# One written order for five engine queues over the first seven attention cycles of a fused attention, layer-norm, MLP and token-mixing kernel

## The chip, the core and the metric

The kernel runs on one core of a Trainium2 chip. The core has a matrix engine (PE, with its weight loads PEld), a vector engine (DVE), an activation engine (ACT), a slower general engine (POOL) and a queue engine (SP) that issues loads and stores. Each engine takes its instructions in the order of its own queue; an instruction that needs the result of another engine waits on a semaphore. The metric is device time in microseconds (us); the median of several runs of the changed kernel is set against 537.79 us.

## What is computed

```python
# attention, 2 batches x 8 heads x 768 positions x 64, fp32
scores = q @ k.T / 8 + bias            # keep: first n_global=8 keys, or the last n_local=96
a = exp(scores - max) / (sum + 1e-9)
x = (a @ v), heads side by side        # 2 x 768 x 512
# layer norm and MLP
x = x + relu(layernorm(x) * g @ w_ch1) @ w_ch2          # 512 -> 2048 -> 512
# mixing
theta = x @ w_theta;  z = x*cos(theta), x*sin(theta)
u = x + w_tok_r @ z_r + w_tok_i @ z_i
out = u + relu(u @ w_ch)
```

All inputs are 32-bit floats, but the weights reach the kernel as 64-bit words in an array `wall`, 58 pieces of 128x512; each piece has to be decoded into a 32-bit tile and then split into a high and a low part for the matrix products of the MLP.

## The kernel before

The 1536 positions are 12 blocks of 128 (`SEQ`, in the order 1, 2, 3, 4, 5, 7, 8, 0, ...). A loop over cycles `t` works on several blocks at once: cycle `t` makes the scores of block `t`, the value product of block `t-1` and its layer norm, and, from cycle 3 on, two hidden tiles of the MLP. So each cycle puts on PE two halves of the scores (`s<-k,q`), four transposes of the probabilities (`pt<-ident,e`), one value product (`xa<-pts,v`), a transpose back (`xp`), one of the normalized block (`xnp`), two hidden products (`hp`) and two output products (`op`). On DVE stand the row maxima (line 229, which adds the bias and keeps the maximum), half of the copies of `pt` to `pts` (line 275), the softmax scale (L311), the layer norm (L323 to L331), the low parts (L341, L438) and two steps of decoding (L374, L375). On ACT stand the exponentials (L236), the other half of the copies (L273), the lift of `xa` (L298), the high parts (L340, L396, L438) and the two other steps of decoding (L369, L373). POOL makes the low parts of the first eight split weight pieces (L397). All heads of a block have to be through maximum, exponential, transpose and copy before its value product can begin.

Eight weight pieces, those of the first four hidden tiles, are decoded and split within the first six cycles (`NPIECES`). From cycle 7 on the loop is the same in both kernels.

What sets the order: in `tc.manual_schedule(engines={...})` the named engines take their instructions as the program is written. In this loop that is PE alone; for DVE, ACT, POOL and SP a scheduler picks at build time, by its own estimates, among what is ready, held by a few hints such as

```python
with tc.issue_after(lifted) if t else ExitStack():
    soften_(t, HI)                       # maxima and exponentials of heads 4 to 7
pieces(want[0])                          # behind_exp: decode behind the last exponential
```

PE starts with 11 products on zeros (`spin`, line 87), and eight more stand in cycle 0 (`idle`, `idle0b`, `idle0c`, from `SPINS`). The bias tiles are made in `make_bias`: a chain of eight DVE steps (L170 to L178), then one scaled copy for each head, two on DVE (`DVE_BIAS`, L183) and six on ACT (L185).

Of the kernel before, what the change touches and what calls it, by code (L numbers as in the profile page):

```python
# [12 lines left out]
U32 = mybir.dt.uint32  # L13
AF = mybir.ActivationFunctionType
# [3 lines left out]
P = 128  # L18
# [25 lines left out]
def kernel(ctx, tc, q, kwin, v, n_pair, g_ln, wall, out):  # L44
# [45 lines left out]
    make_identity(nc, ident)  # L90
# [62 lines left out]
    def make_bias(old):  # L153
# [24 lines left out]
        v_.scalar_tensor_tensor(rel, key, nl, rel, ALU.subtract, ALU.max)  # L178
        for h in range(H):
# [6 lines left out]
        yield  # L186
# [35 lines left out]
    def soften(b, i, p, e, s):  # L222

        nk = e.shape[-1]
        b0 = 0 if i else WIN
        nm, sm = stat[b, i]
        for j in range(2):
# [5 lines left out]
            maxima.append(r.ins)  # L233
        for j in range(2):
# [3 lines left out]
        e_t[b, i, p] = e  # L238

    def scores(b, i, ps_):  # L240

        nk = WIN if i else P
        if ps_[0] == 0:
# [14 lines left out]
    def soften_all(b, i, ps_, s):  # L258
        for a, p in enumerate(ps_):
            e = at.tile([P, 2, s[0].shape[-1]], F32, tag="p", name=f"e{b}_{i}_{p}", bufs=NE)  # L260
            soften(b, i, p, e, [s[j][:, a, :] for j in range(2)])

    def flip_probs(b, i, p):
        nb = 2 if i else 1
        e = e_t.pop((b, i, p))
        pt_tag = "m" if p % 2 else "pt"
        pt = ps(pt_tag, [P, 2, nb, P], f"pt{b}_{i}_{p}")
# [3 lines left out]
        pts = at.tile([P, 2, nb, P], F32, tag="pt", name=f"pts{b}_{i}_{p}", bufs=NPT)  # L271
        if p % 2 == 0:
# [3 lines left out]
        pts_t[b, i, p] = pts  # L276

# [71 lines left out]
    n_staged, n_decoded = [0], [0]  # L349
# [10 lines left out]

    def decode(i, out):

        n = n_decoded[0]
        n_decoded[0] += 1
        load_to(n)
        assert order[n] == i
        r = stage.pop(i)
        load_to(n + NRAW)
        nc.scalar.activation(out, r.bitcast(F32)[:, :, 1], AF.Copy, scale=2.0**-112)  # L369
        t = rawp.tile([P, DM], I32, tag="dec", name=f"dec{i}", bufs=1)  # L370
        o = out.bitcast(I32)
        if i >= 0:
            nc.scalar.activation(t, r.bitcast(U32)[:, :, 0], AF.Copy, scale=2.0**-29 * (1 - 2.0**-15), bias=-0.4999)  # L373
            nc.vector.scalar_tensor_tensor(t, o, 3, t, ALU.logical_shift_left, ALU.bitwise_or)  # L374
            nc.vector.scalar_tensor_tensor(o, r[:, :, 1], -2**31, t, ALU.bitwise_and, ALU.bitwise_or)  # L375
            return
        nc.vector.tensor_scalar(t, o, 3, None, ALU.logical_shift_left)
        nc.vector.scalar_tensor_tensor(t, o, -2**31, t, ALU.bitwise_and, ALU.bitwise_or)
        nc.vector.scalar_tensor_tensor(o, r[:, :, 0], 29, t, ALU.logical_shift_right, ALU.bitwise_or)
# [8 lines left out]
    def split_w(f, ds=(0, 1)):  # L388
        decode_to(2 * f + ds[-1] + 1)
        r = split_t.setdefault(f, [])  # L390
        for d in ds:
            nm = ("w1", "w2")[d]
            s = piece[2 * f + d]
            hi = ws.tile([P, DM], F32R, tag=f"{nm}h", name=f"{nm}h{f}", bufs=GROUP)
            lo = ws.tile([P, DM], F32R, tag=f"{nm}l", name=f"{nm}l{f}", bufs=GROUP)
            nc.scalar.activation(hi, s, AF.Copy)  # L396
            (nc.vector if f >= GROUP else nc.gpsimd).tensor_tensor(lo, s, hi.bitcast(F32), ALU.subtract)  # L397
            r += [hi, lo]
# [5 lines left out]
    def make_xt(t):  # L404
        c, ts = chunk_of[t]
        if c % 2 == 0 and t == ts[0]:
            xt_t[c // 2] = [slot(f"xt{x}{c}") for x in "hl"]
        at_ = c % 2 * CW + ts.index(t) * P
        sl = slice(at_, at_ + P)
        hi, lo = xt_t[c // 2]  # L410
        transposed(xn_t.pop(t), hi[:, :, sl], lo[:, :, sl], "h", f"xnp{t}")
# [5 lines left out]
    def mlp_h(c, f, tag, part=None):  # L417
# [6 lines left out]
        wh, wl = split_t[f][0:2]  # L424
        if part != 1:
            hp_t[c, f] = ps(tag, [P, cn], f"hp{c}_{f}")
        hp = hp_t[c, f]
        kks = range(KD) if part is None else range(part * KD // 2, (part + 1) * KD // 2)
        n = 3 * kks[0]
        for kk in kks:  # L430
# [4 lines left out]
        if part == 0:  # L435
            return
        hh, hl = (act.tile([P, 2 * CW], F32R, tag=f"h{x}", name=f"h{x}{c}_{f}", bufs=2)[:, 0:cn] for x in "hl")
        r = nc.scalar.activation(hh, hp, AF.Relu), nc.vector.scalar_tensor_tensor(hl, hp, 0.0, hh.bitcast(F32), ALU.max, ALU.subtract)  # L438
        relus.append([x.ins for x in r])
        ht_t[c, f] = (hh, hl)  # L440

# [6 lines left out]
    def mlp_o(c, f, fs, js=range(4)):  # L448
# [4 lines left out]
        wh, wl = split_t[f][2:4]  # L453
        for j in js:
# [4 lines left out]
            if f == fs[-1]:  # L459
# [228 lines left out]
    def general():  # L688
# [61 lines left out]
        n_staged[0] = n_decoded[0] = 0  # L750
# [66 lines left out]
    nloaded = [0]  # L817

    def loads_to(n):
        while nloaded[0] <= min(n, len(blocks) - 1):  # L820
            b, i = blocks[nloaded[0]]
            load_qk(b, i)
            load_v(b, i)
            nloaded[0] += 1

    loads_to(0)
    warm = keep.tile([P, 1], F32, name="warm")
    nc.scalar.activation(warm, nhalf, AF.Exp)
    bias_steps = make_bias(True)
    next(bias_steps)  # L830
    next(bias_steps)
    loads_to(1)
    load_to(0)
# [17 lines left out]
    def flips(t, ps_):  # L851
        if 0 <= t < NB:
# [3 lines left out]
    made = []  # L856

    def pieces(n):
        if len(made) < n:
            with behind_exp(len(maxima) - 1):  # L860
                while len(made) < n:
                    m = len(made)
                    split_w(m // 2, (m % 2,))
                    made.append(m)

    sc = {}

    def score(t, ps_):
        if t < NB and (t, ps_) not in sc:
            sc[t, ps_] = scores(*blocks[t], ps_)  # L870

    def soften_(t, ps_):
        if (t, ps_) in sc and sc[t, ps_]:
            soften_all(*blocks[t], ps_, sc[t, ps_])
            sc[t, ps_] = None

    LO, HI = (0, 1), (2, 3)
    with tc.manual_schedule(engines={mybir.EngineType.PE}):
        spin("m", "spin", SPIN0)
        for t in range((LEAD + len(items)) // 2 + 1):  # L880
            j = 2 * t - LEAD
            sp = SPINS[t] if t < len(SPINS) else (0, 0, 0)
            want = NPIECES[min(t, len(NPIECES) - 1)]
            loads_to(t + 2)
            score(t, LO)
            score(t, HI)
            soften_(t, LO)
            if 0 <= t - 1 < NB:
# [3 lines left out]
            with tc.issue_after(lifted) if t else ExitStack():  # L892
# [161 lines left out]
```

## Time and profile before

| | |
|---|---|
| median of three runs | 537.79 us (537.69 to 537.82) |
| profiled execution: its own time | 537.6 us |
| profiled execution: span of the trace | 535.8 us |
| PE busy | 522.2 us, 97% of the span |
| DVE, ACT, POOL busy | 361.0, 284.3, 19.6 us |
| granted clock of PE, mean | 0.999 |

The span runs from the first to the last instruction in the trace; the 1.8 us between it and the time of that execution lie around it. The three runs lie within 0.13 us. A trace time counts from the start of the span.

### The profile page before, as it was taken

The page shows a single profiled execution, that of the slowest core. Times are in us where ns is not written, and L with a number is a line of the kernel's source. Part 1 is how long each engine was busy: PE and PEld are TensorE (multiplying, and loading weights), DVE is VectorE, ACT ScalarE, POOL GpSimd, SP SyncE. Part 2 cuts the span into 40 slices and gives each one's busy share as a digit, 9 for nine tenths or more (in the row PEclk, how much of TensorE's full clock was granted, in tenths as well). Part 3 has the DMA queues.
Part 4 walks back from the last instruction along what each step waited for, and adds up shares of the span by engine and source line. Part 5 has one row for each costly group of instructions (what it writes and reads, how often), then busy time and mean ns, then how long its engine had stood idle before and what let it go on. Part 6 is the DMA issues. An engine that isn't in the chain of part 4 may idle for free.

```text
span 535.8 us, 8220 instructions
## 1 busy us (share of the span) xinstructions
PE 522.2 (97%) x3091; PEld 439.7 (82%) x3091; DVE 361.0 (67%) x789; ACT 284.3 (53%) x631; POOL 19.6 (4%) x32
## 2 busy tenths in 40 slices
PE   8779999999999999999999999999999999999996
PEld 3567889888888888888888887788888888888886
DVE  5898786977774445355468776995996689821532
ACT  6888665667652323332346557972885666620200
POOL 0223100000000000000000000000000000000000
PEclk9999999999999999999999999999999999999999
DMA  8975632312131232012324343221400000000122
GB/s 276 372 236 178 207 110 98 108 53 80 40 120 38 82 105 89 3 40 78 119 78 157 117 159 119 86 72 39 157 2 1 1 0 1 1 1 20 59 81 83
DMA packets 18831, 49.11 MB, mean 92 GB/s; under 512 B 2272, under 2 KB 4576, under 8 KB 18784
## 3 DMA queue, kind: packets, MB, share of 16 engines
q1 hardware_dynamic: 18496, 47.98, 26.4%
q8 instruction: 26, 0.43, 0.3%
q10 hardware_dynamic: 288, 0.52, 0.3%
q14 instruction: 21, 0.17, 0.1%
HBM read 45.35 MB, written 3.15 MB: 91 GB/s over the span
## 4 chain that ended last, share of the span: by engine, by line
PE 90%; ACT 5%; DVE 3%; issue 1%; DMA 1%; ACTq 0%; DVEq 0%
PE op L458 24%; PE hp L433 24%; PE acc L633 19%; PE thm L556 6%; PE ch L679 6%; PE pt L270 3%; PE xa L289 3%; PE s L255 2%; ACT e L236 2%; PE xp L339 1%; PE xp L310 1%; PE xnp L339 1%; DVE w L375 1%; DMA words<-in_n 1%; DVE e L229 1%
## 5 line engine op out<-in xcount | busy, mean ns | idle before, releaser
L633 PE MATMUL acc<-tokh,z 128*128 128x256 f32 (+1 forms) x384 | 95.5, 336 | 0.0
L438 ACT ACTIVATE hh<-hp 128x512 fp32r<-128x512 f32 (+1 forms) x60 | 30.5, 508 | 101.7 <-PE hp L433 101.5
L433 PE MATMUL hp<-xth,w1h 128*128 128x512 f32 (+1 forms) x240 | 84.2, 351 | 0.0
L433 PE MATMUL hp<-xtl,w1h 128*128 128x512 f32 (+1 forms) x240 | 83.2, 347 | 0.0
L433 PE MATMUL hp<-xth,w1l 128*128 128x512 f32 (+1 forms) x240 | 83.1, 346 | 0.0
L458 PE MATMUL op<-w2h,hh 128*128 128x512 f32 x192 | 76.9, 400 | 0.0
L458 PE MATMUL op<-w2l,hh 128*128 128x512 f32 x192 | 75.0, 390 | 0.0
L458 PE MATMUL op<-w2h,hl 128*128 128x512 f32 x192 | 74.8, 392 | 0.0
L633 PEld LDWEIGHTS acc<-tokh,z 128*128 128x128 f32 x384 | 66.6, 190 | 7.9
L438 DVE SCALAR_TENSOR_TENSOR hl<-hp,hh 128x512 fp32r<-128x512 f32 (+1 forms) x60 | 34.7, 579 | 56.3 <-ACT hh L438 56.2
L633 PE MATMUL acc<-tokl,z 128*128 128x512 f32 (+1 forms) x192 | 64.6, 336 | 0.0
L236 ACT ACTIVATE e<-e,nm 128x256 f32<-128x256 f32 (+1 forms) x96 | 45.8, 479 | 15.1 <-DVE nm L229 15.1
L433 PEld LDWEIGHTS hp<-xth,w1h 128*128 128x128 f32 x240 | 45.2, 188 | 7.9 <-ACT e L236 0.9
L433 PEld LDWEIGHTS hp<-xtl,w1h 128*128 128x128 f32 x240 | 45.3, 189 | 6.2 <-DVE xtl L341 0.2
L433 PEld LDWEIGHTS hp<-xth,w1l 128*128 128x128 f32 x240 | 45.3, 189 | 5.6
L458 PEld LDWEIGHTS op<-w2h,hl 128*128 128x128 f32 x192 | 36.0, 188 | 8.5 <-DVE hl L438 0.9
L458 PEld LDWEIGHTS op<-w2l,hh 128*128 128x128 f32 x192 | 36.1, 188 | 6.6
L458 PEld LDWEIGHTS op<-w2h,hh 128*128 128x128 f32 x192 | 36.1, 188 | 6.5
L373 ACT ACTIVATE dec<-raw 128x512 int32<-128x512 uint32 x58 | 38.3, 661 | 4.5 <-DVE chr L375 1.7
L633 PEld LDWEIGHTS acc<-tokl,z 128*128 128x128 f32 x192 | 36.4, 190 | 4.1
L229 DVE CUSTOM_DVE_ANT_0 e<-s,bias 128x256 f32<-128x256 f32 (+1 forms) x96 | 32.4, 395 | 6.0 <-PE s L255 6.0
L446 DVE SCALAR_TENSOR_TENSOR x2all<-op,rsall,x2all 128x512 f32<-128x512 f32 x48 | 33.3, 741 | 2.1 <-PE op L458 2.1
(142 smaller groups left out, 889.4 us busy)
## 6 DMA issues: line engine op xcount, KB each, us to landing
raw<-in_wall SPq DMA_DIRECT2D x58, 512.0 KB, 3.5
k<-in_kwin SPq DMA_DIRECT2D x9, 512.0 KB, 5.2
vc<-in_v SPq DMA_DIRECT2D x12, 256.0 KB, 4.2
q<-in_q SPq DMA_DIRECT2D x11, 256.0 KB, 4.1
out<-o SPq DMA_DIRECT2D x8, 256.0 KB, 2.0
vw<-in_v SPq DMA_DIRECT2D x10, 192.0 KB, 5.2
out<-o SPq DMA_DIRECT2D x8, 128.0 KB, 1.8
vw<-in_v SPq DMA_DIRECT2D x10, 64.0 KB, 4.9
```

The source lines that it names most:

```text
L229: r = nc.vector.tensor_tensor_reduce(out=e[:, j, :], in0=s[j], in1=bias[h][:, b0:b0 + nk], scale=-SCALE, scalar=3.0e38, op0=ALU.add, op1=A ...
L236: r = nc.scalar.activation(e[:, j, :], e[:, j, :], AF.Exp, bias=nm[:, h:h + 1], scale=-1.0, accum_out=sm[:, h:h + 1])
L270: nc.tensor.transpose(pt[:, j, c, :], e[:, j, c * P:(c + 1) * P], ident)
L289: nc.tensor.matmul(xa[j * D:(j + 1) * D, p, :], vv[:, h * D:(h + 1) * D], pts[:, j, c, :], start=(c == 0), stop=(c == nb - 1),)
L373: nc.scalar.activation(t, r.bitcast(U32)[:, :, 0], AF.Copy, scale=2.0**-29 * (1 - 2.0**-15), bias=-0.4999)
L433: nc.tensor.matmul(hp, l, r[:, kk, :], start=(n == 0), stop=(n == 3 * KD - 1))
L438: r = nc.scalar.activation(hh, hp, AF.Relu), nc.vector.scalar_tensor_tensor(hl, hp, 0.0, hh.bitcast(F32), ALU.max, ALU.subtract)
L446: nc.vector.scalar_tensor_tensor(x2[t], o, rsall[:, t:t + 1], x2[t], ALU.mult, ALU.add)
L458: nc.tensor.matmul(op_t[c][j], l, r, start=(f == fs[0] and n == 0), stop=(f == fs[-1] and n == 2))
L556: nc.tensor.matmul(mp, l[:, kk, :], r[:, kk, :], start=(n == 0), stop=(n == 3 * KD - 1))
L633: mm = nc.tensor.matmul(o, l[:, dsl], r[:, sl], start=first and not (paired and d % 2), stop=end and not (paired and d % 2 == 0))
L679: nc.tensor.matmul(mp, l[:, kk, es], r, start=(kk == 0 and m == 0), stop=(kk == KD - 1 and m == 2))
```

## The change

The loop over the first seven cycles is replaced by a list of 283 units, `ORDER`, and all five queues take their instructions in the order of this list. The code of these cycles is cut into the functions that the units name. The letters that the text below uses: S half of a block's scores, M and E maxima and exponentials of two heads, F transpose and C copy of two heads (the last letter of a C says whether ACT, `s`, or DVE, `v`, copies), V value product, L lift, K inverse sum, X transpose back, Y scale, N and J layer norm, T, H and W transpose and high and low part of the normalized block, A, B, D and G the four decoding steps (ACT, ACT, DVE, DVE), I and P high part (ACT) and low part (POOL) of a weight piece, U hidden product, h and l its high and low part, O output product, g its addition to the block, q and v loads, b and f bias steps. The digit behind a letter is the cycle, block, piece or hidden tile; `V3` is the value product of the fourth block in `SEQ`.

```diff
-    make_identity(nc, ident)
...
-DVE_BIAS = 2
-FIRST = 5
-EARLY = 1
-NPIECES = [(0, 1), (1, 3), (3, 5), (5, 8), (8, 8)]
+DVE_BIAS = 4
-SPINS = [(4, 2, 2)]
+ORDER = """
+S00 b0 b3 b1 b2 S01 Z4 M00 E00 M03 M02 E03 F00p M01 S11 E02 C00v E01 F03o M12 F02m C03v F01p C02s K0 E12 S10 C01v
...
@@ make_bias @@
+        nc.gpsimd.iota(rel[:, own], [[-1, P]], base=0, channel_multiplier=1, **io)
         if old:
...
-        nc.gpsimd.iota(rel[:, own], [[-1, P]], base=0, channel_multiplier=1, **io)
...
+    def decode_high(i, out):
+        decode_part(i)["out"] = out
+        nc.scalar.activation(out, stage[i].bitcast(F32)[:, :, 1], AF.Copy, scale=2.0**-112)
+
+    def decode_low(i):
+        t = decode_part(i)["low"] = rawp.tile([P, DM], I32, tag="dec", name=f"dec{i}", bufs=1)
+        nc.scalar.activation(t, stage[i].bitcast(U32)[:, :, 0], AF.Copy, scale=2.0**-29 * (1 - 2.0**-15), bias=-0.4999)
+
+    def decode_merge(i):
+        out, t = (dec_t[i][x] for x in ("out", "low"))
+        nc.vector.scalar_tensor_tensor(t, out.bitcast(I32), 3, t, ALU.logical_shift_left, ALU.bitwise_or)
+
+    def decode_sign(i):
...
+        load_to(order.index(i) + NRAW)
+        nc.vector.scalar_tensor_tensor(out.bitcast(I32), r[:, :, 1], -2**31, t, ALU.bitwise_and, ALU.bitwise_or)
...
-    loads_to(0)
+    qk_to(1)
+    v_to(0)
...
+    with tc.manual_schedule(engines={ET.DVE, ET.Pool}):
+        next(bias_steps[True])
+        make_identity(nc, ident)
+        next(bias_steps[True])
+    with tc.manual_schedule(engines={ET.SP}):
+        load_to(0)
+        qk_to(2)
+        v_to(1)
+        load_to(1)
+        nc.sync.dma_start(gbc, g_ln.partition_broadcast(P))
+        v_to(2)
+        load_to(2)
...
+    with tc.manual_schedule(engines={ET.PE, ET.Activation, ET.DVE, ET.Pool, ET.SP}):
+        spin("m", "spin", SPIN0)
+        for token in ORDER.split():
+            UNITS[token[0]](*[int(x) if x.isdigit() else x for x in token[1:]])
...
     with tc.manual_schedule(engines={ET.PE}):
-        spin("m", "spin", SPIN0)
-        for t in range((LEAD + len(items)) // 2 + 1):
+        for t in range(FIRST, (LEAD + len(items)) // 2 + 1):
```

`FIRST` is 7 in the last line. Three places show what moved. The first is ACT at the start. `bias` tiles are scaled copies, `e` the probabilities of a block and a pair of heads, `warm` a first exponential on one column. Before:

```order
L828 ACTIVATE warm<-nhalf 128x1
L185 ACTIVATE bias_102<-biasTrue_121 128x256
L185 ACTIVATE bias_103<-biasTrue_121 128x256
L185 ACTIVATE bias_104<-biasTrue_121 128x256
L185 ACTIVATE bias_105<-biasTrue_121 128x256
L185 ACTIVATE bias_106<-biasTrue_121 128x256
L185 ACTIVATE bias_107<-biasTrue_121 128x256
L236 ACTIVATE e_1_0_195,sm_1_182<-e_1_0_195,nm_1_181 128x256 x2
```

and now:

```order
L911 ACTIVATE warm<-nhalf 128x1
L193 ACTIVATE bias_100<-biasTrue_123 128x256
L193 ACTIVATE bias_101<-biasTrue_123 128x256
L193 ACTIVATE bias_102<-biasTrue_123 128x256
L193 ACTIVATE bias_103<-biasTrue_123 128x256
L251 ACTIVATE e_1_0_211,sm_1_185<-e_1_0_211,nm_1_184 128x256 x2
L251 ACTIVATE e_1_3_216,sm_1_185<-e_1_3_216,nm_1_184 128x256 x2
```

Two copies of the bias have left ACT for DVE, and the second pair of heads that goes through is pair 3. The second place is ACT around the lift of the first block (`xs_1`), with the second block's probabilities (`e_2`) and the first two weight pieces (`w`, `dec`, `w1h`). Before:

```order
L298 ACTIVATE xs_1_321<-xa_1_304 128x512
L396 ACTIVATE w1h_291<-w_279 128x512
L236 ACTIVATE e_2_2_323,sm_2_236<-e_2_2_323,nm_2_235 128x256 x2
L236 ACTIVATE e_2_3_328,sm_2_236<-e_2_3_328,nm_2_235 128x256 x2
L273 ACTIVATE pts_2_0_354<-pt_2_0_349 128x512
L369 ACTIVATE w_386<-raw_280 128x512
L373 ACTIVATE dec_390<-raw_280 128x512
L273 ACTIVATE pts_2_2_368<-pt_2_2_363 128x512
```

and now:

```order
L251 ACTIVATE e_2_0_302,sm_2_233<-e_2_0_302,nm_2_232 128x256 x2
L321 ACTIVATE xs_1_318<-xa_1_285 128x512
L251 ACTIVATE e_2_3_280,sm_2_233<-e_2_3_280,nm_2_232 128x256 x2
L251 ACTIVATE e_2_1_310,sm_2_233<-e_2_1_310,nm_2_232 128x256 x2
L292 ACTIVATE pts_2_3_354<-pt_2_3_337 128x512
L292 ACTIVATE pts_2_0_360<-pt_2_0_329 128x512
L411 ACTIVATE w_367<-raw_159 128x512
L292 ACTIVATE pts_2_1_377<-pt_2_1_362 128x512
```

The split of the first weight piece (`w1h`) no longer stands between the lift and the exponentials; it comes more than twenty rows later, and ACT copies three pairs of this block. The third place is PE between the first and the second value product (`xa_1`, `xa_2`). Before:

```order
L289 MATMUL xa_1_304<-pts_1_3_268,vc_1_114 64x128 x2
L310 MATMUL xp_335<-ident,xs_1_321 128x128 x4
L270 MATMUL pt_2_0_349<-ident,e_2_0_243 128x128 x4
L270 MATMUL pt_2_1_356<-ident,e_2_1_248 128x128 x4
L270 MATMUL pt_2_2_363<-ident,e_2_2_323 128x128 x4
L270 MATMUL pt_2_3_370<-ident,e_2_3_328 128x128 x4
L339 MATMUL xnp_379<-ident,xn_345 128x128 x4
L255 MATMUL s_3_0_0_421<-k_3_173,q_3_172 128x256
```

and now:

```order
L312 MATMUL xa_1_285<-pts_1_3_259,vc_1_114 64x128 x2
L285 MATMUL pt_2_2_313<-ident,e_2_2_251 128x128 x4
L337 MATMUL xp_322<-ident,xs_1_318 128x128 x4
L285 MATMUL pt_2_0_329<-ident,e_2_0_302 128x128 x4
L285 MATMUL pt_2_3_337<-ident,e_2_3_280 128x128 x4
L269 MATMUL s_3_0_0_348<-k_3_151,q_3_150 128x256
L269 MATMUL s_3_0_1_349<-k_3_151,q_3_150 128x256
L269 MATMUL s_3_0_0_348<-k_3_151,q_3_150 128x256
L269 MATMUL s_3_0_1_349<-k_3_151,q_3_150 128x256
L285 MATMUL pt_2_1_362<-ident,e_2_1_310 128x128 x4
L376 MATMUL xnp_372<-ident,xn_356 128x128 x4
```

A transpose of probabilities stands ahead of the transpose back (`xp`), and half of the third block's scores ahead of the last transpose and of `xnp`.

## Rows read from the trace of the kernel before

**Rows 1.** The page: busy time, share of the span and instructions of PE.

```profile
PE 522.2 (97%) x3091; PEld 439.7 (82%) x3091; DVE 361.0 (67%) x789; ACT 284.3 (53%) x631; POOL 19.6 (4%) x32
```

**Rows 2.** Stretches between value products: start:end, length, busy by engine, clock, DMA, GB/s.

```profile
15.55:26.17 10.62, 7.73 (x74) 6.03 (x73) 9.28 (x25) 9.30 (x25) 2.81 (x3) 1.00 1.04 374
26.17:37.00 10.83, 7.79 (x74) 6.03 (x73) 10.10 (x31) 9.44 (x28) 3.11 (x4) 1.00 0.67 226
37.00:48.81 11.81, 11.45 (x104) 9.70 (x103) 10.34 (x33) 9.67 (x28) 2.62 (x4) 1.00 0.56 190
48.81:62.15 13.34, 12.50 (x110) 10.87 (x108) 11.65 (x35) 9.29 (x27) 4.68 (x6) 1.00 0.63 198
62.15:74.44 12.29, 12.29 (x110) 10.85 (x109) 10.11 (x37) 7.29 (x25) 0.55 (x1) 1.00 0.31 109
...
84.80:535.80 451.00, 446.37 (x2471) 380.30 (x2470) 292.28 (x566) 221.57 (x447) 4.04 (x6) 1.00 0.20 68
```

**Rows 3.** Waits of PE from 5.98 to 84.80: us, times, longest.

```profile
PE xp L310 <- ACT xs L298: 3.1, 3, 1.5
PE pt L270 <- ACT pts L273: 3.0, 3, 1.7
```

**Rows 4.** Two stretches that begin with the first maximum and first exponential.

```profile
7.14:48.81 41.67, 34.72 (x295) 25.72 (x291) 35.95 (x117) 36.57 (x106) 8.54 (x9) 1.00 0.81 282
8.36:48.81 40.45, 33.50 (x286) 25.11 (x284) 34.73 (x111) 35.35 (x102) 8.54 (x9) 1.00 0.80 280
```

**Rows 5.** Waits of ACT from 8.36 to 48.81.

```profile
ACT w2h L396 <- DVE w L375: 2.4, 3, 1.4
ACT e L236 <- DVE nm L229: 1.6, 2, 0.8
```

**Rows 6.** Timeline of DVE and ACT at the start: begin, us, operation.

```profile
4.50 0.22 DVE L170 TENSOR_SCALAR biasTrue<-biasTrue 128x128 f32<-128x128 f32 x1
...
5.08 0.35 DVE L175 TENSOR_SCALAR biasTrue<-biasTrue,nval 128x256 f32<-128x256 f32 x1
...
6.45 0.50 DVE L183 TENSOR_SCALAR bias<-biasTrue 128x256 bf16<-128x256 f32 x2
7.14 0.42 DVE L229 CUSTOM_DVE_ANT_0 e<-s,bias 128x256 f32<-128x256 f32 x1 [0.20 <-PE s L255]
...
6.51 1.95 ACT L185 ACTIVATE bias<-biasTrue 128x256 bf16<-128x256 f32 x6 [3.35 <-DVE biasTrue L178]
8.36 0.49 ACT L236 ACTIVATE e<-e,nm 128x256 f32<-128x256 f32 x1
```

**Rows 7.** Timeline of POOL and DVE where a split meets a decoding step.

```profile
25.20 1.28 POOL L397 TENSOR_TENSOR w2l<-w,w2h 128x512 fp32r<-128x512 f32 x1 [3.09 <-ACT w2h L396]
...
25.72 1.30 DVE L374 SCALAR_TENSOR_TENSOR dec<-w,dec 128x512 int32<-128x512 int32 x1
...
27.29 0.68 DVE L375 SCALAR_TENSOR_TENSOR w<-raw,dec 128x512 int32<-128x512 int32 x1
```

**Rows 8.** Timeline of PE: units of a cycle, and the start of cycle 7.

```profile
64.05 0.39 PE L433 MATMUL hp<-xth,w1h 128*128 128x256 f32 x1
...
65.58 0.60 PE L310 MATMUL xp<-ident,xs 128*128 128x128 f32 x4
...
72.51 2.00 PE L255 MATMUL s<-k,q 64*128 64x256 f32 x16
74.44 0.44 PE L289 MATMUL xa<-pts,vw 128*64 128x128 f32 x4
...
84.80 1.16 PE L255 MATMUL s<-k,q 64*128 64x128 f32 x16
```

**Rows 9.** The first two stretches of 10 us, columns as in rows 2.

```profile
0.00:10.00 10.00, 8.61 (x36) 3.68 (x36) 6.27 (x30) 4.98 (x15) 1.20 (x10) 1.00 0.79 250
10.00:20.00 10.00, 8.59 (x76) 5.86 (x76) 6.85 (x24) 8.86 (x29) 0.96 (x1) 1.00 1.04 373
```

**Rows 10.** Timeline of PE: one of the two later groups of products on zeros, cycle 0.

```profile
11.91 0.61 PE L87 MATMUL idle0b<-zero 128*128 128x512 bf16 x2
```

More of the change, by code (lines that the diff above doesn't have):

```diff
@@ L233, in soften, with exponential @@
             maxima.append(r.ins)
+        e_t[b, i, p] = e
+    def exponential(b, i, p):
+        e = e_t[b, i, p]
+        nm, sm = stat[b, i]
         for j in range(2):
@@ L423, in mlp_h @@
             xh, xl = xt_t[c]
[L424 to L430, printed above, removed]
+        wh, wl = split_t[f, 0]
+        hp = hp_t[c, f] = ps(tag, [P, cn], f"hp{c}_{f}")
+        n = 0
+        for kk in range(KD):
             a, al = wh[:, kk * P:(kk + 1) * P], wl[:, kk * P:(kk + 1) * P]
@@ L458, in mlp_o @@
                 nc.tensor.matmul(op_t[c][j], l, r, start=(f == fs[0] and n == 0), stop=(f == fs[-1] and n == 2))
-            if f == fs[-1]:
+            if f == fs[-1] and add:
                 add_mix(t, op_t[c][j])
@@ L838, with score, add_last, narrow @@
     items = [(c, f) for c in range(NCH) for f in GROUPS[0]]
+    LO, HI = (0, 1), (2, 3)
+    FIRST = 7
+    sc = {}
+    def score(t, g):
+        sc[t, g] = scores(*blocks[t], (LO, HI)[g])
+    def add_last(j):
+        c, f = items[j]
+        for a, t in enumerate(CHUNKS[c]):
+            add_mix(t, op_t[c][a])
+    def narrow(n):
+        if n == 0:
+            bias_steps[False] = make_bias(False)
+            next(bias_steps[False])
+            next(bias_steps[False])
+        else:
+            for _ in range(1 if n < 3 else 2):
+                next(bias_steps[False])
@@ new lines, in high @@
+    def high(m):
+        piece[m] = w_pool.tile([P, DM], F32, tag="w", name=f"w{m}", bufs=NW)
+        decode_high(m, piece[m])
+    UNITS = {
+        "S": score,
+        "M": lambda t, p: maximum(*blocks[t], p, [sc[t, p // 2][j][:, p % 2, :] for j in range(2)]),
+        "E": lambda t, p: exponential(*blocks[t], p),
+        "F": lambda t, p, x: flip_e(*blocks[t], p, {"p": "pt"}.get(x, x)),
+        "C": lambda t, p, x: copy_p(*blocks[t], p, x == "s"),
+        "V": lambda t: [values(*blocks[t], p) for p in ROWS],
+        "L": lambda t: lift_x(*blocks[t]),
+        "K": lambda t: inverse_sum(*blocks[t]),
+        "X": lambda t: flip_xs(*blocks[t], "s"),
+        "Y": lambda t: scale_x(*blocks[t]),
+        "N": lambda t: moments(SEQ[t]),
+        "J": lambda t: center(SEQ[t]),
+        "T": lambda t: flip_xn(SEQ[t], "h"),
+        "H": lambda t: xt_high(SEQ[t]),
+        "W": lambda t: xt_low(SEQ[t]),
+        "A": high,
+        "B": decode_low,
+        "D": decode_merge,
+        "G": decode_sign,
+        "q": qk_to,
+        "v": v_to,
+        "I": lambda m: split_high(m // 2, m % 2),
+        "P": lambda m: split_low(m // 2, m % 2),
+        "U": lambda j: mlp_p(*items[j], "sh"[j % 2]),
+        "h": lambda j: relu_high(*items[j]),
+        "l": lambda j: relu_low(*items[j]),
+        "O": lambda j: mlp_o(*items[j], GROUPS[0], range(2), False),
+        "g": add_last,
+        "b": lambda n: next(bias_steps[True]),
+        "f": narrow,
+        "Z": lambda n: spin("o", "idle", n),
+    }
@@ L851, in flips @@
     def flips(t, ps_):
-        if 0 <= t < NB:
+        if t < NB:
             for p in ps_:
                 flip_probs(*blocks[t], p)
[L856 to L878, printed above, removed]
-        spin("m", "spin", SPIN0)
-        for t in range((LEAD + len(items)) // 2 + 1):
-            j = 2 * t - LEAD
[L882 to L888, printed above, removed]
+    with tc.manual_schedule(engines={ET.PE}):
+        for t in range(FIRST, (LEAD + len(items)) // 2 + 1):
+            j = 2 * t - LEAD
+            qk_to(t + 2)
+            v_to(t + 2)
+            if t < NB:
+                score(t, 0)
+                score(t, 1)
+                soften_all(*blocks[t], LO, sc[t, 0])
+            if t <= NB:
                 for p in ROWS:
@@ L891 @@
                 lifted = lift_x(*blocks[t - 1])
-            with tc.issue_after(lifted) if t else ExitStack():
-                soften_(t, HI)
-            if t == 0:
-                nc.sync.dma_start(gbc, g_ln.partition_broadcast(P))
-            pieces(want[0])
+            if t < NB:
+                with tc.issue_after(lifted):
+                    soften_all(*blocks[t], HI, sc[t, 1])
             if t > NB:
                 down(j - 1)
-            if sp[0]:
-                spin("o", f"idle{t}", sp[0])
             up(j, "s")
-            if 0 < t <= NB:
+            if t <= NB:
                 finish_x(*blocks[t - 1])
@@ L923 @@
                 make_xt(SEQ[t - 1])
-            pieces(want[1])
-            if want[1] == 2 * GROUP and t >= 7:
-                with behind_exp(len(maxima) - 1):
-                    decode_to(2 * GROUP + min(NW, t - 6))
-            if t == FIRST:
-                with behind_exp(len(maxima) - 1):
-                    for _ in make_bias(False):
-                        pass
-            if t == 8:
-                with behind_exp(len(maxima) - 1):
+            with behind_exp(len(maxima) - 1):
+                decode_to(2 * GROUP + min(NW, t - 6))
+                if t == 8:
                     test_n()
```

227 lines of the change are left out of this document (129 added, 98 removed).

## The prediction

> **What bounds the kernel now.** The page comes first: PE is busy 97% of the span [rows 1], so only the remaining 3% and work that is not needed can be won, unless the matrix work itself shrinks, and it doesn't. The second view is busy time by stretches, cut at the value products of successive blocks, which mark the cycles [rows 2]. It shows two regimes. From 15.55 to 48.81 a cycle takes 10.6 to 11.8 us, PE is busy for only 7.7 us in the first two of them, and DVE and ACT are busy 85 to 95% of the time: there the chain runs through DVE and ACT. From 62.15 on PE is busy for the whole 12.29 us of a cycle and the others have slack: there PE is the bound. So what the list can win lies before about 60 us. The third view, PE's waits, names what is late: the transpose back waits for ACT's lift (3.1 us) and transposes wait for ACT's copies (3.0 us) [rows 3]. The last 451 us hold 4.6 us of idle PE that the change doesn't touch [rows 2].
>
> The next question is whether ACT and DVE are full or only badly ordered. Between its first exponential at 8.36 and the fourth value product, V3, at 48.81, ACT is busy 35.35 of 40.45 us; from its first maximum at 7.14, DVE is busy 35.95 of 41.67 [rows 4]. Both have some 5 us of holes, and ACT's largest are waits for DVE: for the end of a decoding (2.4 us) and for maxima (1.6 us) [rows 5]. ACT and DVE hand work to and fro, each time with the wrong piece of work in front. That is what an order can mend, and 5.1 us on ACT is the size of it.
>
> **The change, part by part.** *The start.* DVE now makes four bias copies before the first maximum instead of two; two took 0.50 us [rows 6], so +0.5. The steps L170 and L171, which fill 4.50 to 5.08 behind the arrival of the counts [rows 6], now stand before them, where DVE waits anyway: -0.58. The first maximum stays near 7.14, where it also needs the scores. ACT makes four copies in place of six, which took 1.95 us: -0.65, so its first exponential can start at 7.7; the chain's 0.58 would bring 7.2, but the maximum (0.42 us from 7.14) ends at 7.6. I take 7.65, a gain of 0.7.
>
> *ACT and DVE up to V3.* I counted the units in the list before the copies that V3 waits for (C31v, C30s). ACT has 16 exponential pairs as before, one copy more (+0.48, start to start), one decoding (-0.57) and one high part (-0.55) less: 35.35 - 0.64 = 34.7 us of work. DVE has about 33.8 us: one pair of maxima more, one each of C, D, G, W and l less. From 7.14 DVE could be through at 40.9 and ACT, from 7.65, at 42.35; ACT is the later one. To this come the holes that the list leaves. Bounds: 0, and the 5.1 us of now. I went through the list queue by queue with the durations of the trace. The first value product can begin at 13.1 (now 15.55): the last exponential of block 0 ends at 11.6, its transpose, copy and hand-overs take 1.5. The second comes at about 20 and the third at 30.5 (now 26.17 and 37.00), with ACT nearly full. Two holes show: ACT waits 0.2 for the maxima of M10, and in the fourth cycle DVE's G3 meets the POOL split P2. Rows 7 give the price of such a meeting: the split ran from 25.20 to 26.48, the decoding step that began at 25.72 took 1.30 instead of some 0.68 and ended 0.54 after the split. G3 has the same kind of operands as that step (two, both in on-chip memory), and would begin as P2 begins: up to 1.2 us, behind which M33 and so ACT's E33 wait; no row has a G there, so 0 to 1.2; I take 1.0, as for L374. Holes of 1.2 in all put V3 at 43.55, against 48.81.
>
> The Trainium skill (SBUF — State Buffer, "Who interferes with whom") states it as a rule: a DVE instruction with two SBUF inputs and a GpSimd instruction that reads SBUF exclude each other, and the second to start waits for the first to finish. The trace agrees for L374 (1.30 us) and shows no G or J under a split. By the rule the 1.0 us stays; by the rows alone it could be 0, and the sum 1.0 lower.
>
> *PE from V3 to the end of cycle 6.* Now this takes 84.80 - 48.81 = 35.99 us [rows 2, 8], 0.84 of it idle (12.50 busy of 13.34) [rows 2]. In the list one hidden product (65.58 - 64.05 = 1.53 [rows 8]) has moved ahead of V3 into time that PE had free, and one half of the scores (half of 74.44 - 72.51 = 0.97 [rows 8]) behind it: 35.15 - 1.53 + 0.97 = 34.6. In the fifth cycle two transposes (F50, F53) stand 0.3 each behind their exponentials by the durations: +0.6. The cycle ends at 43.55 + 34.6 + 0.6 = 78.75.
>
> *What costs nothing.* Four of the eight products on zeros are gone (two groups of about 0.6 us [rows 10]); PE waits for exponentials there, which cover it; without that cover they would be 1.2 us of gain already in the 13.1. The granted clock stays at 1.00 through stretches where PE is busy 7.7 of 10.6 us [rows 2], and the list leaves PE busier than that. SP's loads: the list needs the scores' operands, the first weight pieces and the layer norm's factors, 4.7 MB by issue order, before J0 at 18.2. The first 20 us moved 2.5 + 3.7 = 6.2 MB [rows 9], and 4.7 MB were in at about 16, so the loads are covered by 2 us. A weight load waits on SP for the G that frees its buffer and holds up the q, k and v loads behind it; the nearest case, block 3's q and k behind the load that waits for G0 (19.6), lands some 6 us after that, about 2 us before S30. On POOL the splits wait behind the small power steps of J (0.56 us each), with slack. From cycle 7 on the order of all queues is soon the same as before, and PE is the bound, so what is won early stays.
>
> **The sum.** 84.80 - 78.75 = 6.05 us, from 0.7 (start), 3.9 (ACT's holes, 5.1 to 1.2), 0.64 (ACT work moved behind V3), and 0.8 behind V3 (35.99 - 35.2). The profiled execution's own time is 537.6 us, which makes 531.55; the median of the runs lies 0.2 higher, so the forecast is **531.7 us**.
>
> **Rivals.** (1) *The holes stay.* A fixed order can leave as many waits as a scheduler's: V3 = 7.65 + 34.7 + 5.1 = 47.45, then 34.6 + 0.84, end 82.9, gain 1.9, 535.9 us. For it: ACT and DVE need each other in every unit, and each is over 85% busy, so one late unit shifts all behind it. Against it: the largest holes [rows 5] come from a split that stands directly behind its own decoding, and in the list other units stand between. (2) *POOL's splits hold DVE more often.* Three splits stand between V1 and V3 beside DVE's two-operand steps; if each costs its full 1.28 us [rows 7] instead of the 1.0 in the sum, +2.8: 534.5. For it: rows 7. Against it: in my walk P1 falls beside Y1 and N1, which read one operand from on-chip memory. The skill's rule on SBUF named above would make J such a victim too, and this rival is what it gives at most. (3) *Slower: the loads arrive late.* One fixed order waits for the first load that is late, and then all five queues stand. J0 has a cover of 2 us; each further us shifts the whole chain by 1 us, and the kernel is slower than now when those 4.7 MB land after 24.5, that is at under 190 GB/s where rows 9 have 250 and 373: at 28, +3.5 us, 541.3. (4) *No change*, if what is won is lost again, when cycle 7 finds its operands or copies not ready; it would have to wait 6 us, while S7's loads can be issued as soon as S41 has freed the buffers, 30 us earlier.
>
> **How the numbers follow.** Forecast 0.66, rival 1 0.14, rival 2 0.10, rival 3 0.04, rival 4 0.06. At the fast end no hole is left: 7.65 + 34.7 + 34.6 = 76.95, gain 7.85, 529.9; a little less idle at the start could add 0.4. At the slow end stands rival 1. So 529.5 to 535.8. A difference of 0.2%, 1.1 us, is about what a measurement of this kernel tells from no change: faster 0.89 (forecast and rivals 1 and 2, less a little for rival 1's tail), same 0.06, slower 0.05.
>
> **What would show it.** First exponential at 7.5 to 7.8; value products at about 13, 20, 30.5, 43.5, 55 and 66; the scores of cycle 7 at 78.7 with 128-column products; ACT over 93% busy between its first exponential and V3; PE's waits for lifts gone; the stretch behind cycle 7 still 451 us. The prediction is wrong if V2 comes after 33 (ACT or DVE has holes there: look which unit waits), if SP's loads release PE or ACT, or if the granted clock leaves 1.00 in the first 30 us.

## The result, and the profile after

The changed kernel takes 530.94 us (median, 530.69 to 531.23), the kernel before 537.74 us beside it: a ratio of 0.9874, 95% interval [0.9857, 0.9891]. A second series of runs gave 530.87 against 537.78, ratio 0.9872 [0.9857, 0.9887]. The forecast was 531.7 us. The profiled execution took 530.98 us, 529.2 of it span.

The page's first row, and then the stretches between value products, with the columns of [rows 2]:

```profile
PE 521.1 (98%) x3087; PEld 439.6 (83%) x3087; DVE 358.1 (68%) x788; ACT 285.2 (54%) x632; POOL 19.9 (4%) x32
```

```profile
13.20:19.82 6.62, 6.31 (x66) 4.96 (x64) 6.13 (x21) 6.62 (x21) 0.49 (x1) 1.00 0.85 291
19.82:30.71 10.89, 9.16 (x82) 6.67 (x81) 10.72 (x36) 10.89 (x31) 2.64 (x3) 1.00 0.89 302
30.71:42.78 12.07, 12.03 (x107) 10.75 (x106) 11.68 (x38) 11.51 (x32) 5.60 (x5) 1.00 0.85 282
42.78:55.01 12.23, 12.08 (x105) 10.05 (x105) 10.90 (x31) 9.12 (x27) 3.49 (x5) 1.00 0.69 229
55.01:65.41 10.40, 10.34 (x97) 8.94 (x95) 8.06 (x28) 8.28 (x25) 1.82 (x2) 1.00 0.55 178
65.41:78.22 12.81, 12.81 (x108) 11.11 (x106) 8.54 (x34) 8.83 (x29) 0.55 (x1) 1.00 0.31 105
78.22:529.20 450.98, 446.35 (x2471) 380.37 (x2470) 292.43 (x565) 221.68 (x447) 4.04 (x6) 1.00 0.20 68
7.13:42.78 35.65, 33.58 (x294) 26.54 (x290) 34.36 (x117) 34.74 (x101) 8.73 (x8) 1.00 0.89 309
7.59:42.78 35.19, 33.12 (x290) 26.16 (x286) 33.90 (x115) 34.45 (x100) 8.73 (x8) 1.00 0.89 308
```

Everything is won before cycle 7: its scores begin at 78.22 where they began at 84.80, 6.58 us earlier, and the span is 6.6 us shorter. The stretch behind takes 450.98 us, as before (451.00) [rows 2]. The lead is there early: V0 comes 2.35 us sooner than before (13.20 against 15.55), V1 already 6.35 (19.82 against 26.17), V3 6.03. From V0 to V1 ACT has 6.62 us of work where it had 9.30 [rows 2]; what has moved behind V1, such as the first split, fills ACT's holes there: from V1 to V3 it is busy for 22.40 of 22.96 us, where it was 19.11 of 22.64.

The last two rows answer to [rows 4]: from its first exponential to V3, ACT is busy for 34.45 of 35.19 us (98%; it was 87%), DVE from its first maximum for 34.36 of 35.65. Between V1 and V2 ACT doesn't rest at all (10.89 of 10.89), and PE still idles for 1.73 us there.

The waits of PE from 5.9 to 80 us, and those of ACT from 7.6 to 45 us, answer to [rows 3] and [rows 5]:

```profile
PE xnp L376 <- DVE rsall L365: 1.8, 2, 1.6
PE xp L337 <- ACT xs L321: 0.3, 1, 0.3
```

```profile
ACT dec L415 <- DVE w L426: 0.6, 1, 0.6
ACT e L251 <- DVE nm L239: 0.2, 1, 0.2
ACT pts L292 <- PE pt L285: 0.2, 1, 0.2
```

PE's waits for lifts fell from 3.1 to 0.3 us, those for ACT's copies (3.0) are gone, and one wait for the layer norm (1.6) is new. ACT's two waits of [rows 5], 4.0 us together, have become 0.2 (for one maximum); its longest is now one of 0.6 for a decoding step of DVE (G3).

### The profile page after: what moved, and what is told of

Its sections match the earlier page's. It is cut to its first block, busy times and chain, and to the rows that moved or that the text cites. A ratio compares the mean times of both kernels' runs of the same rounds, so it can differ in the third digit from the quotient of the medians.

```text
span 529.2 us, 8191 instructions
## 1 busy us (share of the span) xinstructions
PE 521.1 (98%) x3087; PEld 439.6 (83%) x3087; DVE 358.1 (68%) x788; ACT 285.2 (54%) x632; POOL 19.9 (4%) x32
## 4 chain that ended last, share of the span: by engine, by line
PE 90%; DVE 5%; ACT 2%; DMA 1%; issue 1%; SPq 0%
PE op L537 24%; PE hp L503 24%; PE acc L712 19%; PE thm L635 6%; PE ch L758 6%; PE s L269 3%; PE xa L312 2%; PE pt L285 2%; DVE e L239 2%; DMA k<-in_kwin 1%; DVE w L426 1%; PE xp L376 1%; ACT e L251 1%; PE spin L95 1%; PE xp L337 1%; PE xnp L376 1%
```

## The experiments

Three accounts are set apart. A, the forecast's: the gain lies in the order of ACT's and DVE's work ahead of V3. B: PE's new order carries it, the scheduler would do the rest as well. C: the products on zeros that are gone had a part in it. The start of the trace is not equally long in every execution: in kernels that differ only behind it, the first exponential begins between 7.08 and 8.16. So places in a trace are also compared **from the first exponential on**. In the six traces in which the list sets cycle 0 on all queues, unchanged, V0 comes 5.60 to 5.61 us behind it, and in both traces of the changed kernel cycle 7 comes 70.63 to 70.64 us behind it (before: 76.44). The second of them is from the series of 530.87 us, which ran beside three of the kernels below. The others are set against the changed kernel of another series; the kernel before took 537.73 to 537.78 us in each.

> The changed kernel itself, beside the three that follow, so that they are read against the same chip: 530.7 to 531.3 us by every theory.

**The list for some engines only** (on the others the scheduler picks again):

```diff
-    with tc.manual_schedule(engines={ET.PE, ET.Activation, ET.DVE, ET.Pool, ET.SP}):
+    with tc.manual_schedule(engines={ET.PE}):            # pe_only
+    with tc.manual_schedule(engines={ET.PE, ET.DVE}):    # pe_dve
+    with tc.manual_schedule(engines={ET.PE, ET.Activation}):  # pe_act
```

> The list sets the order on PE alone; on DVE, ACT, POOL and SP the scheduler picks again, now among the small units. Changed kernel: 530.9 us. Theory A (the gain is the written order on ACT and DVE, which closes their holes before the fourth value product): the scheduler leaves holes again, 2 to 4 us of the 6.8 are lost, 532.9 to 534.9. Rival B (cutting the work into units and PE's own new order are enough): 530.5 to 531.5.

> The list sets PE and DVE; ACT, POOL and SP are left to the scheduler. Theory A: the chain of the changed kernel runs on DVE from 10.8 to 35 us, so with DVE fixed only ACT's misplaced units cost, 0.5 to 2 us, 531.4 to 532.9. Rival B: no loss, 530.5 to 531.3.

> The list sets PE and ACT; DVE, POOL and SP are left to the scheduler. Theory A: 1 to 3 us lost, 531.9 to 533.9, since DVE is now the engine on the chain. Rival B: no loss, 530.5 to 531.3.

Measured: PE alone 543.79 us, ratio 1.0111 [1.0094, 1.0128]; PE and DVE 542.88, 1.0102 [1.0085, 1.0119]; PE and ACT 534.92, 0.9949 [0.9932, 0.9966]. Two of them are slower than the kernel before. B falls; but A too had expected all three faster. The waits of ACT from 7 to 60 us and ACT's timeline with the list on PE alone show the reason for the slowest (with PE and DVE the same wait takes 4.0 us):

```profile
ACT dec L415 <- DMA raw<-in_wall: 3.8, 1, 3.8
```

```profile
5.77 1.33 ACT L193 ACTIVATE bias<-biasTrue 128x256 bf16<-128x256 f32 x4 [2.61 <-DVE biasTrue L185]
10.94 0.66 ACT L415 ACTIVATE dec<-raw 128x512 int32<-128x512 uint32 x1 [3.84 <-DMA raw<-in_wall]
11.51 0.49 ACT L251 ACTIVATE e<-e,nm 128x256 f32<-128x256 f32 x1
```

The scheduler put the first decoding ahead of the first exponential. ACT stood there for 3.84 us until the weight piece had landed, and the first exponential came at 11.51. From there to cycle 7 another 79.94 us pass, against 70.63 with the whole list; PE idles, and its granted clock falls, as the second stretch of 10 us of this kernel shows (0.66, third number from the right):

```profile
10.00:20.00 10.00, 7.77 (x46) 5.79 (x48) 4.33 (x16) 7.89 (x28) 0.00 (x0) 0.66 1.04 367
```

With the list on PE and ACT this doesn't happen: in that trace no wait of PE, ACT, DVE or POOL for a load is listed from 5 to 90 us, and the granted clock stays at 1.00 through the first 80 us. Still 4.0 us of the gain are lost. Of ACT's waits from 12 to 70 us the largest is for maxima, which the changed kernel hardly has:

```profile
ACT e L251 <- DVE nm L239: 3.7, 2, 2.4
```

So an order for PE and ACT is not enough while the scheduler orders DVE.

**That mishap taken out.** The list for PE alone again, but decoding and high parts are held behind the last maximum and the last exponential that stand ahead of them in the list:

```diff
-    with tc.manual_schedule(engines={ET.PE, ET.Activation, ET.DVE, ET.Pool, ET.SP}):
+    with tc.manual_schedule(engines={ET.PE}):
...
+            with ExitStack() as es:
+                if token[0] in "ABDGI":
+                    es.enter_context(tc.issue_after(maxima[-1]))
+                    es.enter_context(tc.issue_after(exps[-1]))
```

> The list for PE alone; for ACT, DVE, POOL and SP the scheduler picks, but the decoding and the splits are held behind the last maximum and exponential that stand ahead of them in the list. A (an order for ACT and DVE is needed throughout): 532 to 536 us. B (what the list on PE alone lost was only the decoding that stood ahead of the exponentials and waited 3.8 us for its load): 530.5 to 531.5 us, with no wait of ACT for a raw load over 1 us.

Measured: 536.42 us, 0.9971 [0.9958, 0.9983]. So holding decodings and splits back returns 7.4 us of what the list on PE alone lost, and the 5.5 that remain against the changed kernel lie in the order of the other queues, SP's loads among them. In its trace, from an execution of 535.45 us, 3.2 us are lost from V0 to V3 (32.76 us instead of 29.58) and 1.7 from there to cycle 7. The waits from 12 to 70 us are many and small, as in the kernel before; of PE, and of ACT:

```profile
PE xnp L376 <- DVE rsall L365: 2.9, 2, 2.1
PE xp L337 <- ACT xs L321: 2.1, 3, 1.5
PE pt L285 <- ACT pts L292: 1.0, 1, 1.0
```

```profile
ACT e L251 <- DVE nm L239: 1.8, 3, 1.0
ACT w L411 <- DMA raw<-in_wall: 1.7, 2, 1.2
```

B falls; A holds in kind, with a time 0.4 past its slow edge. Waits for loads are still there (1.7 us, one of 1.2). The scheduler's order here is one of many; another might lose less.

**The start alone**, put into the kernel before: four bias copies on DVE, the count first on POOL, and the first steps of the bias in written order.

```diff
-DVE_BIAS = 2
+DVE_BIAS = 4
...
+    with tc.manual_schedule(engines={mybir.EngineType.DVE, mybir.EngineType.Pool}):
+        next(bias_steps)
+        make_identity(nc, ident)
+        next(bias_steps)
```

> The kernel before with the new start alone: four bias copies on DVE, the two early bias steps ahead of the counts, the new order of POOL's first steps. Before: 537.7. Theory A (the first exponential comes 0.7 earlier, and ACT carries that to V3): 537.0. Rival E (the old order's holes swallow it): 537.5 to 537.8.

Measured: 537.17 us against 537.78 (10 and 19 runs), 0.9988 [0.9978, 0.9997], 0.61 us won (0.2 to 1.2 by the interval). In its trace V0 is at 15.03, 7.19 us behind the first exponential, just as far as before (8.36 to 15.55).

**The products on zeros**, once out of the kernel before, once back into the changed one (Z2 is a group of two):

```diff
-SPINS = [(4, 2, 2)]
+SPINS = [(4, 0, 0)]
```

```diff
-... M01 S11 E02 C00v E01 F03o M12 F02m C03v F01p C02s K0 E12 S10 C01v
+... M01 S11 Z2 E02 C00v E01 F03o M12 F02m C03v F01p C02s K0 E12 S10 Z2 C01v
```

> The kernel before without the two later groups of products on zeros in cycle 0. Theory A (PE waits for exponentials there anyway): 537.2 to 537.8. Rival C (they are 1.2 us on the chain): 536.5.

> The changed kernel with the four dropped products on zeros put back, two behind S11 and two behind S10. Theory A (PE waits in cycle 0, so they are covered): 530.9 to 531.5; the second pair stands right ahead of V0 and can cost up to 0.5. Rival C (their removal is a real part of the gain): plus 1.1, 532.0.

Measured: without them the kernel before takes 537.15 us against 537.78, 0.9989 [0.9980, 0.9999]; with them the changed kernel takes 532.04 us, 0.9895 [0.9878, 0.9911]. C is right in kind: they were not all covered, though the kernel before wins only 0.63 us, half of C's 1.2. From first exponential to V0 the kernel before needs 6.64 us without them, where it needed 7.19; the changed kernel needs 6.54 with them, where it needs 5.61. PE's timeline of the kernel before, with them and then without them, shows which group it is:

```profile
15.02 0.60 PE L87 MATMUL idle0c<-zero 128*128 128x512 bf16 x2
15.55 0.44 PE L289 MATMUL xa<-pts,vw 128*64 128x128 f32 x4
```

```profile
12.94 1.09 PE L270 MATMUL pt<-ident,e 128*128 128x128 f32 x8 [0.94 <-ACT pts L273]
...
15.02 0.44 PE L289 MATMUL xa<-pts,vw 128*64 128x128 f32 x4
```

Ahead of the transposes at 12.94 PE now waits 0.94 us, where it waited 0.41 behind the group that stood in this gap [rows 10]: that group was free. The other group stood at 15.02 directly ahead of V0, which was ready, and cost 0.53 (15.55 to 15.02).

**A hole put back ahead of V2.** Weight piece 1 is merged, signed and split in one go, so that ACT's split stands directly behind DVE's two steps, the pattern of [rows 5]:

```diff
-V1 B1 W0 E20 M21 E21 D1 S21 G1 L1 F21o M22 I1 v3 ...
+V1 B1 D1 G1 I1 W0 E20 M21 E21 S21 L1 F21o M22 v3 ...
```

> The changed kernel with one pattern of the old order put back once: the high part of weight piece 1 (I1) directly behind its own decoding (B1 D1 G1 I1, ahead of W0, E20, M21). ACT then stands from the end of B1 until G1 is done, some 1.3 us. Theory A (ACT and DVE are full up to V3, so a hole there goes into the end one for one): plus 1.0 to 1.4, 531.9 to 532.3. Rival D (slack behind it takes it up): plus 0.3 at most, up to 531.2.

Measured: 533.09 us, 0.9913 [0.9897, 0.9930]. ACT's timeline there:

```profile
20.88 0.68 ACT L415 ACTIVATE dec<-raw 128x512 int32<-128x512 uint32 x1
23.04 0.63 ACT L445 ACTIVATE w2h<-w 128x512 fp32r<-128x512 f32 x1 [1.49 <-DVE w L426]
```

The hole is 1.49 us, and V2 comes 12.59 us behind V1 instead of 10.89. Of these 1.70 us 1.64 are still there at cycle 7 (72.27 us from the first exponential, against 70.63). D falls; A's mechanism is right, its range too low. The time in the runs grew by 2.15. In the profiled execution (533.07 us) the first exponential also came 0.47 us later than in that of the changed kernel (8.06 against 7.59), which makes up the rest; whether the other executions had this too is not known.

**The same hole behind V3**, with weight piece 7, where PE is busy for 12.08 of 12.23 us:

```diff
-... C41s D7 O2 H3 ... M52 G7 F50p L4 M53 U4 I7 E53 P7 ...
+... C41s D7 G7 I7 O2 H3 ... M52 F50p L4 M53 U4 E53 P7 ...
```

> The two DVE steps and the high part of weight piece 7 stand directly behind one another, as a hole of ACT, but between V3 and V4, where PE is busy throughout. A (only holes ahead of V3 count, PE bounds behind it): +0 to +0.3, 530.9 to 531.2 us. B (any hole of ACT in the first seven cycles goes into the end): +1.3, 532.2 us.

Measured: 532.30 us, 0.9899 [0.9884, 0.9914], 1.43 more than the changed kernel beside it (530.87). That looks like B's one for one, but the trace splits it. From V3 to cycle 7, 0.85 us are lost, where A allowed 0.3: A falls. ACT waits 0.99 us for its split:

```profile
52.44 0.63 ACT L445 ACTIVATE w2h<-w 128x512 fp32r<-128x512 f32 x1 [0.99 <-DVE w L426]
```

With it H3, W3, the last copy ahead of V4, the maxima and E50 come later, E50 by 1.3 us counted from V3, so that V4 is 0.46 late and PE then waits 0.45 for E50. So there were some 0.5 us in hand (1.3 less 0.85), not a whole cycle's slack. The chain that ended last in the changed kernel (start, us, what; rows left out at the dots) agrees:

```profile
38.72 7.05 DMA k<-in_kwin
...
58.16 0.36 ACT w2h L445
58.70 1.09 ACT e L251 x4
59.83 0.44 PE pt L285 x2
```

It passes from DVE and ACT to PE only at 59.83, between V4 and V5, and not at V3 (42.78), although PE shows next to no wait in between. (The load from 38.72 to 45.77 is an inferred link. The decoding step that it is said to release began where DVE's step ahead of it ended, at 45.02 + 0.69 = 45.71, so no wait for this load is shown.) The rest was lost earlier, in a stretch that the edit doesn't touch: from V1 to V2, 11.82 us instead of 10.88, of which 0.33 are made good by V3. PE's timeline there in this kernel, and in the changed kernel measured beside it:

```profile
26.83 0.66 PE L376 MATMUL xnp<-ident,xn 128*128 128x128 f32 x4 [1.63 <-DVE xn L364]
...
27.85 3.51 PE L269 MATMUL s<-k,q 64*128 64x256 f32 x16
```

```profile
27.33 0.66 PE L376 MATMUL xnp<-ident,xn 128*128 128x128 f32 x4 [1.63 <-DVE xn L364]
...
28.35 2.57 PE L269 MATMUL s<-k,q 64*128 64x256 f32 x16
```

The same wait, the same products, but 3.51 us instead of 2.57. Stretches of 1 us in the first of the two kernels say why (the third column from the right is the granted clock):

```profile
28.00:29.00 1.00, 1.00 (x6) 0.83 (x8) 1.00 (x3) 1.00 (x3) 0.00 (x0) 0.58 1.06 322
29.00:30.00 1.00, 1.00 (x8) 0.90 (x6) 0.56 (x2) 1.00 (x3) 0.00 (x0) 0.50 0.97 385
30.00:31.00 1.00, 1.00 (x8) 0.56 (x4) 1.00 (x5) 1.00 (x3) 0.54 (x1) 0.50 0.99 340
```

Behind the wait of 1.63 us the clock fell to its lower level for some 3.4 us (2.4 GHz is 1.00, 1.2 GHz is 0.50). In the changed kernel it stays at 1.00 behind a wait of the same length. This is one execution: in the four runs the mean clock is 0.996 to 0.998 and the time 532.00 to 532.59, in no common order, so the clock's share of the 1.43 us is not shown for all of them. The kernel with the products on zeros put back lost 1.1 us in the same way, between V1 and V2, in its profiled execution, and made 0.4 of it good by V3.

**The layer norm's factors late**: gbc is issued behind block 3's v and the third weight piece.

```diff
-        nc.sync.dma_start(gbc, g_ln.partition_broadcast(P))
         v_to(2)
         load_to(2)
+        nc.sync.dma_start(gbc, g_ln.partition_broadcast(P))
```

> The layer norm's factors are loaded behind block 3's v and the third weight piece, so that they land some 2.6 us after J0's time. A (the loads' cover is the 1.2 us that the trace shows, and what exceeds it goes into the end): 532.4 to 533.5 us, with DVE waiting for gbc. B (slack behind J0 takes it up): at most +0.5, 530.9 to 531.4 us.

Measured: 534.41 us, 0.9938 [0.9924, 0.9951], 3.54 more than the changed kernel, which took 530.87 beside it. DVE's timeline, and two stretches behind:

```profile
18.16 0.18 DVE L358 BATCH_NORM_AGGREGATE mv<-bn 128x2 f32<-128x6 f32 x1
20.71 0.75 DVE L364 SCALAR_TENSOR_TENSOR xn<-x2all,mv,gbc 128x512 f32<-128x512 f32 x1 [2.37 <-DMA gbc<-in_g_ln]
```

```profile
21.00:22.00 1.00, 0.48 (x4) 0.42 (x4) 1.00 (x3) 0.00 (x0) 0.39 (x1) 1.00 0.00 0
...
23.00:24.00 1.00, 1.00 (x13) 1.00 (x12) 1.00 (x6) 1.00 (x4) 0.00 (x0) 0.50 0.79 205
```

DVE waits 2.37 us, V1 comes 2.33 us later from V0, and with the clock at 0.50 behind PE's idle time V2 comes another 1.17 us later from V1; nothing is made good afterwards. A's mechanism is right; its range is too low, because the clock adds half as much again.

**DVE's step out from under the split.** G3 goes behind M33, and B4 behind E33:

```diff
-... M30 E32 G3 P2 U0 M33 L2 q5 B4 K2 E33 D4 ...
+... M30 E32 P2 U0 M33 G3 L2 q5 K2 E33 B4 D4 ...
```

> The changed kernel with G3 behind M33 and B4 behind E33, so that nothing on DVE's way to M33 waits for the POOL split P2 (G3 took 1.73 us there in place of 0.68). Theory A (this wait is on the chain to V3): minus 0.5 to 1.0, 529.9 to 530.4. Rival D (PE or a load is the bound by then): 530.6 to 531.2.

Measured: 531.76 us, 0.9887 [0.9871, 0.9904]: no gain, and neither A nor D has the time. It is 0.8 us slower than the changed kernel of the other series, with overlapping intervals (0.4 in the traces, counted from the first exponential to cycle 7). First the changed kernel (POOL, DVE, ACT), then this one (POOL, DVE):

```profile
30.83 2.53 POOL L450 TENSOR_TENSOR w1l<-w,w1h 128x512 fp32r<-128x512 f32 x2 [2.62 <-ACT w1h L445]
...
31.83 0.42 DVE L239 CUSTOM_DVE_ANT_0 e<-s,bias 128x256 f32<-128x256 f32 x1
32.18 1.73 DVE L426 SCALAR_TENSOR_TENSOR w<-raw,dec 128x512 int32<-128x512 int32 x1
...
33.94 0.69 ACT L415 ACTIVATE dec<-raw 128x512 int32<-128x512 uint32 x1 [0.56 <-DVE w L426]
```

```profile
31.39 2.54 POOL L450 TENSOR_TENSOR w1l<-w,w1h 128x512 fp32r<-128x512 f32 x2 [2.61 <-ACT w1h L445]
...
33.44 1.04 DVE L426 SCALAR_TENSOR_TENSOR w<-raw,dec 128x512 int32<-128x512 int32 x1
...
35.53 0.69 DVE L419 SCALAR_TENSOR_TENSOR dec<-w,dec 128x512 int32<-128x512 int32 x1 [0.74 <-ACT dec L415]
```

G3 still met the end of the split (1.04), and D4 then waited 0.74 for B4, which had been moved behind E33. ACT lost its wait of 0.56 and was 0.59 us ahead at its copy C30s, counted from the first exponential (41.70 - 8.16 against 41.72 - 7.59). Then it waited for the load of weight piece 7, which it doesn't in the changed kernel:

```profile
43.42 0.69 ACT L411 ACTIVATE w<-raw 128x512 f32<-128x512 f32 x1 [1.12 <-DMA raw<-in_wall]
```

And from V2 to V3 there was next to nothing to win on PE, which in the changed kernel is busy for 12.03 of 12.07 us, as D had it. Other waits took the place of the first, so what the meeting costs at the end is not isolated. A second tile for what B writes, which would free ACT of G3, was not tried.

## Why the prediction was right

**The sum**, term by term, with the durations of the two profiled executions:

| term | predicted | measured |
|---|---|---|
| start | 0.7 | 8.36 - 7.59 = 0.77 |
| ACT's holes up to V3 | 5.1 - 1.2 = 3.9 | 5.10 - 0.74 = 4.36 |
| ACT's work moved behind V3 | 0.64 | 35.35 - 34.45 = 0.90 |
| behind V3 | 0.8 | 35.99 - 35.44 = 0.55 |
| sum | 6.05 | 6.58 |

The measured column only splits the two traces into ACT's busy and idle time; that the order of ACT and DVE is the cause rests on the experiments.

The value products came at 13.20, 19.82, 30.71, 42.78, 55.01 and 65.41, forecast at 13.1, 20, 30.5, 43.55, 55 and 66, and cycle 7 at 78.22 instead of 78.75. So the gain was foreseen by its causes, with errors of up to 0.5 us a term, one of them the other way.

*Start.* Right; the start alone is worth 0.61 us in the runs. The single trace says less, since the first exponential moves by a us from one execution to the next.

*Holes up to V3.* Right in place and kind. Put back, one of them costs its full length, 1.70 us for 1.49 (hole1), and with the list on PE alone 5.5 of the 6.9 us are lost (pe_held). The 1.4 us that stay are about what the start (0.61) and the products on zeros (0.63) are worth in the kernel before. Rival 1 gave 535.9 us for holes that stay; with the scheduler's holes it is 536.42. Two readings were less exact. ACT and DVE were not 85 to 95% busy throughout: from 37.00 to 48.81 ACT was at 82%, and PE at 97% [rows 2]. And the forecast took ACT for the later of the two; DVE is nearly as full (34.36 of 35.65 us), and with ACT's order kept and DVE's not, 4.0 us are lost (pe_act).

*G3 under the split P2.* Forecast 1.0, measured 1.73 - 0.68 = 1.05, and it ended 0.55 behind the split, as in [rows 7] (0.54). But behind it waited ACT's B4, whose tile G3 has to free, and not E33 by way of M33: 0.56 of ACT's 0.74 us of holes. That it would shift V3 is not borne out: from V2 to V3 PE was busy for 12.03 of 12.07 us, and V3 came at 42.78 and not at 43.55. A second, smaller meeting was not forecast (D5 at 42.20, 0.89 us). The rule that the prediction cites from the Trainium skill (SBUF — State Buffer, "Who interferes with whom") agrees with the trace: G3 was held (1.73 and, in the other order, 1.04 us), while the maximum that ran under the split just before it, with its scores in PE's result memory, took its usual 0.42. Rival 2 didn't come.

*Behind V3.* PE's work was under-sized, 35.23 us and not 34.6, and the two waits of 0.3 came to 0.2 in all. That PE alone is the bound from V3 on was too early by a cycle and a half. PE has no idle time to speak of from V2 on, but a hole of ACT behind V3 still cost 0.85 us (hole_late), and the chain leaves ACT and DVE only at 59.83. It did no harm, because the list has ACT and DVE in time, with some 0.5 us in hand.

*What costs nothing.* Here a step failed: "PE waits for exponentials there, which cover it" holds for the first of the two groups on zeros, not for the second, which cost 0.53 us ahead of V0. The sum was not harmed, because V0 was worked out without them. The loads' cover was said to be 2 us. gbc was issued at 10.28, landed 6.9 us later and was wanted at 18.43, so it was 1.2; late_g shows that the whole chain stands behind it, as rival 3 had it. The granted clock stayed at 1.00 in the profiled execution, as forecast, but the reason given does not carry it: the list leaves PE busier on average, and with a wait of 1.6 us in one place, behind which the clock fell in two kernels with the same wait. In part this was luck; one of the four runs has a mean clock of 0.994 (531.23 us, the slowest).

The one variant that was to be faster than the changed kernel, nolock, was not.

## What to carry to other kernels

Where two engines are each 80 to 95% busy and hand work to and fro, count their holes up to the point where a third engine becomes the bound. Here that was the size of what an order could win (5.1 us of holes on ACT, 4.4 of them closed), and it had to be written for all the queues: for PE alone it lost 6 us. Ahead of an engine's critical work, nothing in its queue should wait for a load; here one such wait held ACT for 3.84 us. Products that keep PE busy were free where PE waited, and cost 0.53 us directly ahead of a product that was ready.

## What the runs showed of the hardware

A late operand can cost more than its lateness. In late_g, PE's 2.3 us of idling were followed by some 3.4 us at a granted clock of 0.50, worth 1.17 us more. It isn't certain: the wait of 1.63 us between V1 and V2 was followed by 1.00 in both traces of the changed kernel and in nolock, and by 0.50 in two others. The length of the wait doesn't settle it either. With the list on PE and ACT a wait of 2.79 us, longer than that of late_g (2.32), was followed by 1.00:

```profile
29.21 0.66 PE L376 MATMUL xnp<-ident,xn 128*128 128x128 f32 x4 [2.79 <-DVE rsall L365]
```

```profile
30.00:40.00 10.00, 9.01 (x91) 8.10 (x89) 8.53 (x25) 8.72 (x25) 2.97 (x2) 1.00 0.71 250
```

These rows don't tell why. Differences of a microsecond between kernels here carry this with them.

A decoding step of DVE that met a split already under way on POOL ended 0.54 to 0.55 us behind the split's end, in all of its seventeen meetings in eight traces, whether it had begun early or late in the split (it took 0.89 to 1.73 us instead of 0.68). The maximum under the same split in the rows above, with one operand in PE's result memory, took its usual 0.42.
